# Seven small reorderings in a convolution and MLP-mixer kernel: token load order, weight passes, swap copies, output stores and background work

## Chip, cores and metric

The kernel runs on one core of a Trainium2 chip. The metric is the device time of one execution in microseconds (us), the median of several runs. Smaller is better.

## What is computed

The input x has 8 batches of 4096 tokens with 192 channels. A causal convolution with 7 taps per head (8 heads of 24 channels, taps passed through a softmax) goes first, and an MLP mixer follows:

```python
out = np.einsum('hk,bskhg->bshg', w, x_unf)            # convolution over tokens, softmaxed taps
xt = x.transpose(0, 2, 1)                              # x is now the convolution's output
h = np.maximum(xt @ w_tok1, 0.0) @ w_tok2              # token mixing: 4096 -> 256 -> 4096
u = x + h.transpose(0, 2, 1)
h2 = np.maximum(u @ w_ch1, 0.0) @ w_ch2                # channel mixing: 192 -> 1536 -> 192
return (u + h2).astype(np.float32)
```

The weights come in as 64-bit floats and are decoded on the chip into fp32 values. Products keep fp32 precision by a split: each operand is a high and a low part, and hi x hi, hi x lo and lo x hi are summed in PSUM.

## The kernel before, in words

**Groups and tiles.** Batches go in the groups [0], [1], [2, 3], [4, 5], [6, 7] (`GROUPS`, line 16). A group's tokens are cut into 8 spans of 512 tokens (`NT`), each of 4 blocks of 128 (`TJ`). In the groups of two batches, "pair groups" below, a span gives one tile per batch, worked one after the other as a pair.

**One tile.** The second token product (`mix2`) and the convolution's output give `u`. `u` is transposed into `own_hi` and `own_lo`, channels on partitions. Product 1 (`channel1`, matmuls in `channel1_mm`, line 1240) has 6 passes p of 18 matmuls on half the array each (108 in all). Each pass fills two PSUM tiles; ScalarE writes `hh`, the relu'd high part (line 1284), VectorE the low part `hl` (line 1285), and that frees the two PSUM tiles for a later pass. Product 2 has four blocks j: `channel2` (lines 1321, 1322) or, on half arrays, `channel2_halves` (line 1302). After each block VectorE adds products and `u` into `osb` (lines 1327, 1328, or 1308, 1310). `store_out` (line 1335) then sends `osb`, 384 KB for the tile, from POOL's queue. There is one `osb` buffer: the next tile's first write to it waits for the store to land.

**The pair's transposes** go by DMA. `blocks_sent` sends 16 block copies (line 1180). `parted` then casts the three chunks into `own_hi` (line 1192, ScalarE) and `own_lo` (line 1194, VectorE). It also makes a version with its halves of 64 partitions swapped: two ScalarE copies of 64x1536 (line 1197, high part, then low part) and two DMAs on POOL's queue (line 1199). Product 1 takes its weights' two half arrays from `own` and the swapped copy. A POOL memset (line 816) follows each load of raw input.

**Background.** While a group is mixed, the next group is convolved and sent through its first token product. A planner (`Background`, line 35) puts these instructions among the foreground's. `fg(pe, dve, after)` adds a foreground step's planned cost and fills in background items; `after` (600 unless given) says how far VectorE's plan may run ahead of TensorE's. Taps of the convolution are line 824 (first tap, ScalarE) and line 826 (the others, VectorE); raw loads are line 814, loads of decoded token weights line 877 (`t1_load`), stores of convolved tokens line 860. `bg.lands` plans when a load has landed.

**The start.** The first tiles of batch 0 run while weights are decoded on VectorE and ScalarE (lines 199 to 241): `begin(n)` starts the load of piece n, `chains[n]` are its decode steps, `split(n)` gives the high part (ScalarE) and the low part (VectorE). `hooks[0]` is the first tile's second token product. `load_tile` issues the loads of the next tile's `u` (line 1050) on SP's queue.

Of the kernel before, what the change touches and what calls it, by code (L numbers as in the profile page):

```python
# [142 lines left out]
def conv_mixer_kernel(ctx: ExitStack, tc: tile.TileContext, x, weight, w_tok1, w_tok2, w_ch1, w_ch2, out):  # L143
# [26 lines left out]
    def f32(ap):  # L170
        return ap.bitcast(F32)
# [169 lines left out]
    def woven(*lists):  # L341

        lists = [list(v) for v in lists]
        while any(lists):
            for v in lists:
                if v:
                    v.pop(0)()
# [95 lines left out]
    def stage1_first(pe, p0, p1, pd, late, load_u, after, pieces, hooks):  # L443
# [221 lines left out]
        def split(n):  # L665
            jb = jobs[n]
            hi, lo = jb["make"]() if "make" in jb else (jb["hi"], jb["lo"])
            return dec.b(sts[n], hi, lo, jb.get("view", lambda v: v))

        next_load()  # L670
        x0_load(0)
# [57 lines left out]
        low = split(N1)  # L729
        woven(chains[N1 + 1][:2])  # L730
        woven(low)
        held = []
        begin(N1 + 2, held)
        hooks[0]([lambda: None, lambda: None, chains[N1 + 1][2]])
        woven(chains[N1 + 1][3:])
        woven(chains[N1 + 2][:1])
        next_load()
        xc_store(1)
# [52 lines left out]
    def stage1(gi, pools):  # L791
# [44 lines left out]
        def begin(q2, part):  # L836
            def fn():
                states[q2]["raw", part] = load(q2, part)
                if nb > 1:
                    done["load", q2, part] = bg.lands(9e3)  # L840
                else:
                    mark("load", q2, part)

            bg.transfer(fn)
# [143 lines left out]
        convolving.append(Item(lambda: begin(0, 0), eager=True))  # L988
        second = [Item(lambda: begin(0, 1), eager=True, gate=lambda: None if pools(1) is None else 0.0)]
        for n in range(AHEAD[nb]):  # L990
            mixing.append(Item(lambda n=n: t1_load(n), eager=True))
        for q2 in range(NS):

            tap(q2, 0, 0)
# [114 lines left out]
    def mix2_half(t2, u, j, turned):  # L1109

        n = 2 * D
        pss = [ps_x.tile([P, TT], F32, name="ps_x") for _ in range(2)]
        prods = [(kc, r, v) for kc in range(KC) for r, v in ((0, 0), (0, 1), (1, 0))]
        for m, (kc, r, v) in enumerate(prods):
            for k, ps in enumerate(pss):
                ks = slice(k * D2, (k + 1) * D2)
                nc.tensor.matmul(  # L1117
                    out=ps[:, :n], lhsT=t2[ks, kc, r, j, :], rhs=h1[ks, kc, v, :n], start=m == 0, stop=m == len(prods) - 1
                )
        bg.fg(1040, 1070, 200)  # L1120
        uj = u[:, j]
        for ps in pss:
            v = ps[:, :n].rearrange("p (b c d) -> p c b d", b=2, d=D2)
            nc.vector.tensor_tensor(out=uj, in0=v, in1=uj, op=ALU.add)
        turn_blocks(uj, turned, j)
# [58 lines left out]
    def parted(place, other):  # L1184


        own = own_tile("hi"), own_tile("lo")
        low, high = slice(0, D2), slice(D2, P)
        for c in range(ND):
            v = f32(place[:, c]).rearrange("p (i j e) -> p j i e", i=NQ, e=QB)  # L1190
            hi, lo = (o[:, c].rearrange("p (j i e) -> p j i e", i=NQ, e=QB) for o in own)
            nc.scalar.copy(out=hi, in_=v)
            bg.fg(0, 700, 0)
            nc.vector.tensor_tensor(out=lo, in0=v, in1=f32(hi), op=ALU.subtract)
        swapped = other[:, 0], other[:, 1]
        for k in range(2):
            nc.scalar.copy(out=swapped[k][high], in_=f32(own[k][low]))  # L1197
        for k in range(2):
            nc.gpsimd.dma_start(out=f32(swapped[k][low]), in_=f32(own[k][high]))
        return [(own, swapped), (swapped, own)]  # L1200
# [71 lines left out]
    def channel1(t):  # L1272
        h = {}
        for f0 in range(0, NF, NF // 3):
            for n in ("hh", "hl"):
                part = hp.tile([P, NF // 3, TT], F32R, name=f"{n}{f0}")
                for f in range(NF // 3):
                    h[n, order[f0 + f]] = part[:, f]
        bg.tiled = True
        for p in range(NP):  # L1280
            pss = channel1_mm(t, p)
            bg.fg(2040 if p else 2400, 1300)
            for f, ps in pss:
                nc.scalar.activation(out=h["hh", f], in_=ps, func=AF.Relu)  # L1284
                nc.vector.scalar_tensor_tensor(  # L1285
                    out=h["hl", f], in0=ps, scalar=0.0, in1=f32(h["hh", f]), op0=ALU.max, op1=ALU.subtract
                )
        bg.tiled = False
        return h
# [182 lines left out]
    for gi, bs in enumerate(GROUPS):  # L1472
# [13 lines left out]
        for q in range(NT):  # L1486
            nxt = (gi, q + 1) if q + 1 < NT else (gi + 1, 0)
            for i, b in enumerate(bs):
# [30 lines left out]
                if spread and not turn:  # L1519

                    def after(j, z=spread[0], place=spread[1], t2=loaded[0], v=loaded[1]):
                        if j == 1:
                            bg.hold()
                        mix2_half(t2, v, j, z)
                        if j == TJ - 1:
                            blocks_sent(z, place)
                            bg.release()

                    channel2_halves(i, h, u, osb, range(TJ), after)
                    store_out(gi, b, q, osb, range(TJ), nc.gpsimd)  # L1530
                    continue
                if spread:
                    made = []
# [27 lines left out]
                product2 = channel2 if turn or last and q + 1 == NT and i + 1 == nb else channel2_halves  # L1561
                if ahead:
                    product2(i, h, u, osb, half[0])
                if turn and not pairs and ahead:
                    abc, rest = transposed_once(loaded[1])
                run_ahead(gi)
                if last and q + 1 == NT and i + 1 == nb:
                    for j in range(TJ):
                        if j in half[1]:
                            channel2(i, h, u, osb, [j])  # L1570
                        store_out(gi, b, q, osb, range(j, j + 1), nc.sync)
                else:
                    if ahead:
                        if turn and pairs:
                            made = []
                            channel2(i, h, u, osb, half[1], ((half[1][0], 7), lambda: made.extend(parted(other[:, 1], other))))
                            abc = made
                        elif turn:
                            channel2(i, h, u, osb, half[1], ((half[1][0], 7), rest))
                        else:  # L1580
                            product2(i, h, u, osb, half[1])
                    else:
                        made = []
                        first_channel2(u, osb, [3], (NF // 3, lambda: made.extend(transposed(loaded[1]))))
                        abc = made
                        second_split()
                        first["parted"] = 0.0
                        bg.dve = max(bg.dve, bg.pe) + 6e3

                    store_out(gi, b, q, osb, range(TJ), nc.gpsimd if ahead else nc.scalar)  # L1590
                if not ahead:
                    ht_ctx.close()
                    hp = ctx.enter_context(tc.tile_pool(name="hp", bufs=1, reuse_waits="tile"))
                if turn:
                    u = loaded[1]
                    if nxt[1] + 1 < NT:
                        loaded = load_tile(nxt[0], nxt[1] + 1, sp)


# [29 lines left out]
```

## Time and profile before

| | us |
|---|---|
| median of 3 runs (2006.88 to 2008.21) | 2007.21 |
| profiled execution, time | 2009.77 |
| profiled execution, span | 2008.0 |
| TensorE busy in the span | 1999.5 |
| VectorE busy | 1506.4 |
| ScalarE busy | 787.9 |
| POOL busy | 213.6 |

The granted clock of TensorE has the mean 1.0 over the span. Busy times are of the profiled execution and overlap: TensorE is busy nearly all the time, so only its few pauses can be won or lost, and the span is read as TensorE's work plus those pauses.

### The profile page before, as it was taken

To read this page: it belongs to the slowest core of one execution; us is meant where nothing else is said; L and a number is where in the kernel's file an instruction comes from. 1 tells how busy PE (TensorE), PEld (TensorE's weight loads), DVE (VectorE), ACT (ScalarE), POOL (GpSimd) and SP (SyncE) were. 2 spreads that over 40 slices of the span, in tenths; PEclk is the share of its full clock that TensorE was granted. 3 is DMA by queue.
4 is the path that set the end of the run, shared out by engine and by line. 5 is a ranking of instruction groups with operands and counts; after the bars stand their busy time and mean duration, and the time that the engine had idled before them with its cause. 6 is when DMAs were issued, how large, how long until landed. Compare 5 with 4: busy or idle time off the path is not lost.

```text
span 2008.0 us, 45327 instructions
## 1 busy us (share of the span) xinstructions
PE 1999.5 (100%) x19007; PEld 1853.6 (92%) x19007; DVE 1506.4 (75%) x3020; ACT 787.9 (39%) x1310; POOL 213.6 (11%) x376
## 2 busy tenths in 40 slices
PE   9999999999999999999999999999999999999999
PEld 9899999999988999998999999999999999999998
DVE  6899989999558999757888789556666666666664
ACT  7667544444343343323333433333233322333322
POOL 1000000000011101111101110111111110011110
PEclk9999999999999999999999999999999999999999
DMA  9956455553354567515346544433323222333310
GB/s 305 298 155 219 142 173 175 172 191 134 114 160 121 143 176 205 157 58 140 84 129 189 140 128 115 137 87 86 85 63 82 71 66 63 82 85 85 85 48 17
DMA packets 281792, 259.26 MB, mean 129 GB/s; under 512 B 190084, under 2 KB 231620, under 8 KB 281588
## 3 DMA queue, kind: packets, MB, share of 16 engines
q1 hardware_dynamic: 258404, 172.85, 30.6%
q0 software_dynamic: 22656, 83.12, 13.6%
q8 instruction: 150, 2.46, 0.5%
q14 instruction: 54, 0.44, 0.1%
q10 hardware_dynamic: 528, 0.39, 0.1%
HBM read 147.25 MB, written 71.30 MB: 109 GB/s over the span
## 4 chain that ended last, share of the span: by engine, by line
PE 92%; DVE 4%; DMA 2%; ACT 1%; SPq 1%; issue 0%; POOL 0%; DVEq 0%; ACTq 0%; POOLq 0%
PE ps_x L1240 37%; PE ps_x L1302 25%; PE ps_x L1321 10%; PE ps_x L1322 5%; PE ps_x L1117 3%; PE ps_a L932 2%; PE ps_a L933 2%; PE ps_a L934 2%; PE ps_x L1087 1%; PE ps_a L928 1%; DVE xc L826 1%; PE ps_x L1090 1%; DMA dec_raw<-in_moe_w_tok_dram 1%; PE ps_x L1092 1%; PE ps_x L1091 1%; PE ps_x L1161 1%
## 5 line engine op out<-in xcount | busy, mean ns | idle before, releaser
L1284 ACT ACTIVATE hh<-ps_x 128x512 fp32r<-128x512 f32 x756 | 410.2, 595 | 834.1 <-PE ps_x L1240 834.1
L1285 DVE SCALAR_TENSOR_TENSOR hl<-ps_x,hh 128x512 fp32r<-128x512 f32 x756 | 484.6, 686 | 172.1 <-ACT hh L1284 171.6
L1302 PE MATMUL ps_x<-w,hh 64*128 64x384 f32 x3648 | 523.5, 355 | 0.0
L1302 PE MATMUL ps_x<-w,hl 64*128 64x192 f32 x3648 | 462.3, 247 | 0.1
L1240 PE MATMUL ps_x<-other,w_hi 64*128 64x512 f32 x1728 | 448.7, 388 | 0.6 <-ACT other L1197 0.3
L826 DVE SCALAR_TENSOR_TENSOR xc<-raw,cw,xc 128x384 f32<-128x384 f32 (+1 forms) x768 | 389.1, 562 | 9.9 <-ACT xc L824 9.9
L1302 PEld LDWEIGHTS ps_x<-w,hl 64*128 64x128 f32 x3648 | 356.5, 188 | 2.1 <-DVE hl L1285 0.6
L1302 PEld LDWEIGHTS ps_x<-w,hh 64*128 64x128 f32 x3648 | 350.5, 184 | 1.5
L1240 PE MATMUL ps_x<-own_hi,w_hi 64*128 64x512 f32 x1440 | 348.7, 392 | 1.6 <-ACT w_hi L240 0.7
L1321 PE MATMUL ps_x<-w,hh 128*128 128x384 f32 x1200 | 348.1, 361 | 0.0
L1240 PEld LDWEIGHTS ps_x<-other,w_hi 64*128 64x128 f32 x1728 | 315.1, 184 | 32.6 <-ACT other L1197 1.0
L1240 PE MATMUL ps_x<-own_hi,w_lo 64*128 64x512 f32 x1440 | 343.2, 387 | 0.0
L1240 PE MATMUL ps_x<-own_lo,w_hi 64*128 64x512 f32 x1440 | 342.8, 387 | 0.2 <-ACT own_lo L1168 0.2
L1322 PE MATMUL ps_x<-w,hl 128*128 128x192 f32 x1200 | 300.4, 250 | 0.0
L1240 PEld LDWEIGHTS ps_x<-own_hi,w_hi 64*128 64x128 f32 x1440 | 214.7, 184 | 31.9 <-issue 4.2
L1240 PEld LDWEIGHTS ps_x<-own_lo,w_hi 64*128 64x128 f32 x1440 | 219.4, 184 | 26.7 <-ACT own_lo L1168 0.6
L1240 PEld LDWEIGHTS ps_x<-own_hi,w_lo 64*128 64x128 f32 x1440 | 219.3, 184 | 26.0
L1240 PE MATMUL ps_x<-other,w_lo 64*128 64x512 f32 x864 | 242.0, 386 | 0.0
L1322 PEld LDWEIGHTS ps_x<-w,hl 128*128 128x128 f32 x1200 | 229.1, 191 | 0.0
L1321 PEld LDWEIGHTS ps_x<-w,hh 128*128 128x128 f32 x1200 | 225.3, 188 | 0.5 <-DVE hl L1285 0.4
L1310 DVE TENSOR_TENSOR osb<-ps_x,osb 128x192 f32<-128x192 f32 x456 | 163.1, 358 | 26.8 <-DVE osb L1310 0.5
L1240 PEld LDWEIGHTS ps_x<-other,w_lo 64*128 64x128 f32 x864 | 159.0, 184 | 16.2
(190 smaller groups left out, 2025.5 us busy)
## 6 DMA issues: line engine op xcount, KB each, us to landing
raw<-in_x_dram SPq DMA_DIRECT2D x56, 672.0 KB, 8.1
t<-t2d SPq DMA_DIRECT2D x64, 512.0 KB, 5.4
out_dram<-osb POOLq DMA_DIRECT2D x62, 384.0 KB, 4.1
xcd<-xc POOLq DMA_DIRECT2D x28, 768.0 KB, 8.2
u<-xcd SPq DMA_DIRECT2D x56, 384.0 KB, 5.8
t<-t1p SPq DMA_DIRECT2D x32, 512.0 KB, 6.2
other<-own_hi POOLq DMA_DIRECT2D x24, 384.0 KB, 4.0
other<-own_lo POOLq DMA_DIRECT2D x24, 384.0 KB, 3.7
```

The costliest lines, as they stand in the source:

```text
L826: nc.vector.scalar_tensor_tensor(out=dst, in0=src, scalar=cw[:, h, k:k + 1], in1=dst, op0=ALU.mult, op1=ALU.add)
L932: nc.tensor.matmul(out=ps, lhsT=wh, rhs=xh, start=a, stop=False)
L933: nc.tensor.matmul(out=ps, lhsT=wh, rhs=xl, start=False, stop=False)
L934: nc.tensor.matmul(out=ps, lhsT=wl, rhs=xh, start=False, stop=z)
L1117: nc.tensor.matmul(out=ps[:, :n], lhsT=t2[ks, kc, r, j, :], rhs=h1[ks, kc, v, :n], start=m == 0, stop=m == len(prods) - 1)
L1240: nc.tensor.matmul(out=ps, lhsT=w1[w][rows, chunks[h][c], p * P:(p + 1) * P], rhs=t[h][v][rows, c], start=n == 0, stop=n == len(prods) - 1,)
L1284: nc.scalar.activation(out=h["hh", f], in_=ps, func=AF.Relu)
L1285: nc.vector.scalar_tensor_tensor(out=h["hl", f], in0=ps, scalar=0.0, in1=f32(h["hh", f]), op0=ALU.max, op1=ALU.subtract)
L1302: nc.tensor.matmul(out=ps[:, :m], lhsT=h[part, f][ks, ts], rhs=w2[ks, f, :m], start=n == 0 and part == "hh", stop=z and part == "hl",)
L1310: nc.vector.tensor_tensor(out=osb[:, j], in0=v, in1=osb[:, j], op=ALU.add)
L1321: nc.tensor.matmul(out=ps[:, :2 * D], lhsT=h["hh", f][:, ts], rhs=w2[:, f, :], start=n == 0, stop=False)
L1322: nc.tensor.matmul(out=ps[:, :D], lhsT=h["hl", f][:, ts], rhs=w2[:, f, :D], start=False, stop=z)
```

## The change

**A.** The third piece of the channel weights (`split(N1 + 2)`) is cast to its high part in two halves of its columns instead of in one cast. **B.** The first tile's second token product (`hooks[0]`) is issued before the third piece's decode begins, and not woven with it. **C.** For the first raw loads of the last group the planner takes 12 us to landing instead of 9. **D.** The first five loads of token weights for batch 1 (`t1_load`) wait, in the order of issue, until the third tile's tokens have been issued. **E.** The swapped high part is copied in three chunks of 64x512 instead of one copy of 64x1536, and the first pass of product 1 takes its matmuls chunk by chunk (hi x hi, hi x lo of a chunk, then all lo x hi). **F.** In product 1 of pairs the planner's `after` is 300 instead of 600. **G.** In pair groups the output of the pair's first tile, and in the last groups a tile that has the next pair's token product inside it, is stored in two halves of 192 KB, the first one after block j = 1.

```diff
--- before.py
+++ after.py
@@ -665,7 +665,13 @@
             hi, lo = jb["make"]() if "make" in jb else (jb["hi"], jb["lo"])
-            return dec.b(sts[n], hi, lo, jb.get("view", lambda v: v))
+            view = jb.get("view", lambda v: v)
+            if n != N1 + 2:
+                return dec.b(sts[n], hi, lo, view)
+            v = view(sts[n]["top"])
+            for cs in (slice(0, P), slice(P, 2 * P)):
+                nc.scalar.copy(out=hi[:, :, cs], in_=v[:, :, cs])
+            return [lambda: nc.vector.tensor_tensor(out=lo, in0=v, in1=f32(hi), op=ALU.subtract)]
 
@@ -729,10 +735,10 @@
         woven(low)
+        hooks[0]([])
         held = []
         begin(N1 + 2, held)
-        hooks[0]([lambda: None, lambda: None, chains[N1 + 1][2]])
-        woven(chains[N1 + 1][3:])
+        woven(chains[N1 + 1][2:])
         woven(chains[N1 + 2][:1])
@@ -837,7 +843,7 @@
                 if nb > 1:
-                    done["load", q2, part] = bg.lands(9e3)
+                    done["load", q2, part] = bg.lands(12e3 if gi == 4 and not q2 else 9e3)
                 else:
@@ -988,7 +994,7 @@
         for n in range(AHEAD[nb]):
-            mixing.append(Item(lambda n=n: t1_load(n), eager=True))
+            mixing.append(Item(lambda n=n: t1_load(n), eager=True, gate=lambda: first.get("later")))
         for q2 in range(NS):
@@ -1193,8 +1199,9 @@
         swapped = other[:, 0], other[:, 1]
-        for k in range(2):
-            nc.scalar.copy(out=swapped[k][high], in_=f32(own[k][low]))
+        for c in range(ND):
+            nc.scalar.copy(out=swapped[0][high, c], in_=f32(own[0][low, c]))
+        nc.scalar.copy(out=swapped[1][high], in_=f32(own[1][low]))
         for k in range(2):
@@ -1278,8 +1285,8 @@
         for p in range(NP):
-            pss = channel1_mm(t, p)
-            bg.fg(2040 if p else 2400, 1300)
+            pss = channel1_mm(t, p, by_chunk=not p and len(t) == 2)
+            bg.fg(2040 if p else 2400, 1300, 600 if t[0] is t[1] else 300)
             for f, ps in pss:
@@ -1522,12 +1529,14 @@
                         mix2_half(t2, v, j, z)
+                        if j == TJ // 2 - 1:
+                            store_out(gi, b, q, osb, half[0], nc.gpsimd)
                         if j == TJ - 1:
...
                     channel2_halves(i, h, u, osb, range(TJ), after)
-                    store_out(gi, b, q, osb, range(TJ), nc.gpsimd)
+                    store_out(gi, b, q, osb, half[1], nc.gpsimd)
                     continue
@@ -1561,6 +1570,8 @@
                     product2(i, h, u, osb, half[0])
+                    if turn and pairs:
+                        store_out(gi, b, q, osb, half[0], nc.gpsimd)
                 if turn and not pairs and ahead:
@@ -1587,7 +1598,8 @@
 
-                    store_out(gi, b, q, osb, range(TJ), nc.gpsimd if ahead else nc.scalar)
+                    js = half[1] if turn and pairs else range(TJ)
+                    store_out(gi, b, q, osb, js, nc.gpsimd if ahead else nc.scalar)
                 if not ahead:
@@ -1595,6 +1607,8 @@
                         loaded = load_tile(nxt[0], nxt[1] + 1, sp)
+                    if not ahead:
+                        first["later"] = 0.0
```

SP's queue at the start of batch 0's third tile (`raw` is raw input of the next batch, `u` the third tile's tokens, `t` token weights), before:

```order
L262 DMA dec_raw<-in_moe_w_tok_dram 128x1024 x2
L814 DMA raw_788<-in_x_dram 128x14x96
L814 DMA raw_791<-in_x_dram 128x14x96
L877 DMA t_794<-t1d 128x512
L877 DMA t_796<-t1d 128x512
L877 DMA t_798<-t1d 128x512
L877 DMA t_800<-t1d 128x512
L877 DMA t_802<-t1d 128x512
L1050 DMA u<-xcd_75 128x192 x4
L262 DMA dec_raw<-in_moe_w_tok_dram 128x1024 x3
```

and with the change:

```order
L262 DMA dec_raw<-in_moe_w_tok_dram 128x1024 x2
L820 DMA raw_789<-in_x_dram 128x14x96
L820 DMA raw_792<-in_x_dram 128x14x96
L1056 DMA u<-xcd_75 128x192 x4
L883 DMA t_947<-t1d 128x512
L883 DMA t_949<-t1d 128x512
L883 DMA t_951<-t1d 128x512
L883 DMA t_953<-t1d 128x512
L883 DMA t_955<-t1d 128x512
L262 DMA dec_raw<-in_moe_w_tok_dram 128x1024 x3
```

The four loads of `u` go ahead of the five loads of `t`. Lines have shifted by 6.

VectorE in the first pair's second tile, from the first write to `osb` to block j = 2 of product 2 (the bracket lists the semaphores that an instruction waits for; DMASW are POOL's DMAs), before:

```order
L1308 TENSOR_TENSOR osb<-ps_x,u 128x192 [waits DMASW4_49,PE_49]
L1310 TENSOR_TENSOR osb<-ps_x,osb 128x192 [waits DVE_49]
L1310 TENSOR_TENSOR osb<-ps_x,osb 128x192 [waits DVE_49,PE_49]
L1310 TENSOR_TENSOR osb<-ps_x,osb 128x192 [waits DVE_49]
L826 SCALAR_TENSOR_TENSOR xc_6810<-raw_6615,cw,xc_6810 128x16x24 x2
L826 SCALAR_TENSOR_TENSOR xc_6810<-raw_6615,cw,xc_6810 128x16x24 [waits DVE_49] x2
L1308 TENSOR_TENSOR osb<-ps_x,u 128x192 [waits PE_49]
L1310 TENSOR_TENSOR osb<-ps_x,osb 128x192 [waits DVE_49]
L1310 TENSOR_TENSOR osb<-ps_x,osb 128x192 [waits DVE_49,PE_49]
...
L826 SCALAR_TENSOR_TENSOR xc_6810<-raw_6615,cw,xc_6810 128x16x24 x2
L1308 TENSOR_TENSOR osb<-ps_x,u 128x192 [waits PE_49]
```

and with the change:

```order
L1315 TENSOR_TENSOR osb<-ps_x,u 128x192 [waits DMASW5_49,DMASW2_49,PE_49]
L1317 TENSOR_TENSOR osb<-ps_x,osb 128x192 [waits DVE_49]
L1317 TENSOR_TENSOR osb<-ps_x,osb 128x192 [waits DVE_49,PE_49]
L1317 TENSOR_TENSOR osb<-ps_x,osb 128x192 [waits DVE_49]
L832 SCALAR_TENSOR_TENSOR xc_6814<-raw_6616,cw,xc_6814 128x16x24 x2
L832 SCALAR_TENSOR_TENSOR xc_6814<-raw_6616,cw,xc_6814 128x16x24 [waits DVE_49] x2
L1315 TENSOR_TENSOR osb<-ps_x,u 128x192 [waits PE_49]
...
L832 SCALAR_TENSOR_TENSOR xc_6814<-raw_6616,cw,xc_6814 128x16x24 x2
L832 SCALAR_TENSOR_TENSOR xc_6814<-raw_6616,cw,xc_6814 128x16x24 [waits DVE_49] x2
L1315 TENSOR_TENSOR osb<-ps_x,u 128x192 [waits PE_49]
```

The first write to `osb` waits for both halves of the store before it, in place of one store, and two more taps (line 826, 832 with the change) stand ahead of block j = 2.

VectorE two pairs later, from the casts of the low part to the first pass of product 1, before:

```order
L1194 TENSOR_TENSOR own_lo<-other,own_hi 128x512 [waits Activation_49] x2
L826 SCALAR_TENSOR_TENSOR xc_8386<-raw_8344,cw,xc_8386 128x16x24 x2
L1327 TENSOR_TENSOR osb<-ps_x,u 128x192 [waits PE_49]
L1328 TENSOR_TENSOR osb<-ps_x,osb 128x192 [waits DVE_49]
L826 SCALAR_TENSOR_TENSOR xc_9176<-raw_9012,cw,xc_9176 128x16x24 [waits DMAHW1_49,DMAHW0_49,Activation_49]
...
L1327 TENSOR_TENSOR osb<-ps_x,u 128x192 [waits PE_49]
L1328 TENSOR_TENSOR osb<-ps_x,osb 128x192 [waits DVE_49]
L916 TENSOR_TENSOR xhl<-xc_8386,xhl 128x768
L826 SCALAR_TENSOR_TENSOR xc_9176<-raw_9012,cw,xc_9176 128x16x24 x2
L1285 SCALAR_TENSOR_TENSOR hl_9209<-ps_x,hh_9208 128x512 [waits Activation_49] x4
```

and with the change:

```order
L1200 TENSOR_TENSOR own_lo<-other,own_hi 128x512 [waits Activation_49] x2
L1334 TENSOR_TENSOR osb<-ps_x,u 128x192 [waits PE_49]
L1335 TENSOR_TENSOR osb<-ps_x,osb 128x192 [waits DVE_49]
L832 SCALAR_TENSOR_TENSOR xc_9189<-raw_9024,cw,xc_9189 128x16x24 [waits DMAHW1_49,DMAHW0_49,Activation_49]
L832 SCALAR_TENSOR_TENSOR xc_9189<-raw_9024,cw,xc_9189 128x16x24 [waits Activation_49]
...
L1334 TENSOR_TENSOR osb<-ps_x,u 128x192 [waits PE_49]
L1335 TENSOR_TENSOR osb<-ps_x,osb 128x192 [waits DVE_49]
L922 TENSOR_TENSOR xhl<-xc_8361,xhl 128x768
L1292 SCALAR_TENSOR_TENSOR hl_9222<-ps_x,hh_9221 128x512 [waits Activation_49] x2
L832 SCALAR_TENSOR_TENSOR xc_9189<-raw_9024,cw,xc_9189 128x16x24 x2
L1292 SCALAR_TENSOR_TENSOR hl_9222<-ps_x,hh_9221 128x512 [waits Activation_49] x2
```

Two taps behind the casts and two ahead of the first pass's `hl` are gone from here; of the four `hl` of two passes, two now go before the next taps.

## Rows read from the trace of the kernel before

**Rows 1.** The page, part 4.
```profile
PE 92%; DVE 4%; DMA 2%; ACT 1%; SPq 1%; issue 0%; POOL 0%; DVEq 0%; ACTq 0%; POOLq 0%
```

**Rows 2.** The chain that ended last; start us, us, what ran or landed.
```profile
102.47 4.70 DMA u<-xcd
...
602.08 6.81 PE ps_x L1302 x96
...
620.73 8.68 PE ps_x L1240 x71
...
1534.06 12.28 PE ps_x L1240 x108
```

**Rows 3.** Timeline of SP's queue at 92 to 105 us; start us, us, instruction.
```profile
91.91 4.67 SPq L814 DMA_DIRECT2D raw<-in_x_dram  x2
96.62 5.75 SPq L877 DMA_DIRECT2D t<-t1d  x5
102.47 2.03 SPq L1050 DMA_DIRECT2D u<-xcd  x4
```

**Rows 4.** Timeline of VectorE at four places; brackets: idle before, releaser.
```profile
107.27 0.36 DVE L1102 TENSOR_TENSOR u<-ps_x,u 128x192 f32<-128x192 f32 x1 [1.93 <-DMA u<-xcd]
...
608.89 0.36 DVE L1308 TENSOR_TENSOR osb<-ps_x,u 128x192 f32<-128x192 f32 x1 [2.75 <-PE ps_x L1302]
...
616.30 0.75 DVE L1310 TENSOR_TENSOR osb<-ps_x,osb 128x192 f32<-128x192 f32 x2 [0.46 <-DVE osb L1310]
...
781.70 1.14 DVE L826 SCALAR_TENSOR_TENSOR xc<-raw,cw,xc 128x384 f32<-128x384 f32 x2
782.76 2.48 DVE L1285 SCALAR_TENSOR_TENSOR hl<-ps_x,hh 128x512 fp32r<-128x512 f32 x4
```

**Rows 5.** Timeline of TensorE at 59 to 128 us.
```profile
59.89 0.98 PE L1240 MATMUL ps_x<-own_hi,w_hi 64*128 64x512 f32 x6 [0.72 <-ACT w_hi L240]
...
94.85 1.56 PE L1240 MATMUL ps_x<-own_hi,w_hi 64*128 64x512 f32 x6 [0.34 <-DVE hl L1285]
...
118.77 0.73 PE L1240 MATMUL ps_x<-own_hi,w_hi 64*128 64x512 f32 x4
...
127.59 0.62 PE L1240 MATMUL ps_x<-own_hi,w_hi 64*128 64x512 f32 x2
```

**Rows 6.** Timeline of TensorE at 647 to 924 us.
```profile
647.77 0.49 PE L1240 MATMUL ps_x<-other,w_hi 64*128 64x512 f32 x1
...
712.53 0.50 PE L1240 MATMUL ps_x<-other,w_hi 64*128 64x512 f32 x1
...
783.50 0.48 PE L1240 MATMUL ps_x<-own_hi,w_hi 64*128 64x512 f32 x1
784.09 0.50 PE L1240 MATMUL ps_x<-other,w_hi 64*128 64x512 f32 x1
...
922.66 0.36 PE L1302 MATMUL ps_x<-w,hh 64*128 64x384 f32 x2
...
923.90 0.88 PE L1117 MATMUL ps_x<-h,t 64*128 64x384 f32 x8
```

**Rows 7.** Timeline of ScalarE at six places.
```profile
73.53 1.15 ACT L199 ACTIVATE t_first<-dec_raw 128x1024 f32<-128x1024 f32 x1 [3.21 <-DMA dec_raw<-in_moe_w_tok_dram]
...
119.73 0.62 ACT L1167 CAST own_lo<-own_lo 64x512 fp32r<-64x512 f32 x1
...
586.30 1.66 ACT L1192 CAST own_hi<-other 128x512 fp32r<-128x512 f32 x3 [14.38 <-DMA other<-own_hi]
...
646.25 1.48 ACT L1197 CAST other<-own_hi 64x1536 fp32r<-64x1536 f32 x1
...
706.79 1.47 ACT L1197 CAST other<-own_lo 64x1536 fp32r<-64x1536 f32 x1
...
920.65 1.12 ACT L824 ACTIVATE xc<-raw,cw 128x384 f32<-128x384 f32 x2 [1.57 <-POOL raw L816]
```

**Rows 8.** DMA issues from 595 to 599 us; KB each, us to landing.
```profile
out_dram<-osb POOLq DMA_DIRECT2D x1, 384.0 KB, 11.8
```

## Prediction

> **What bounds the kernel now.** I read the chain of waits first. It lies on TensorE for 92% of the span [rows 1], and late in the run its pieces are whole products: a product 1 of 108 matmuls in 12.28 us, 0.1137 us each [rows 2]. That is the pace without a pause, so nothing gains there. What the change can win is the pauses of TensorE in the first half. I looked for them by comparing starts in TensorE's timeline with this pace, and then read the timeline of the engine each pause waits for. Five places matter, and each is met by one or two of the seven edits. The reader should see in the rows who was late there.
>
> - **At 119 to 128 us** 66 matmuls run between two starts, 118.77 and 127.59 [rows 5]. At the pace they take 7.50, so 1.32 us are pauses. VectorE is in arrears there since 107.27, where it had stood for 1.93 us until the third tile's `u` landed [rows 4]. That landing is in the chain [rows 2], and its issue on SP stands behind five loads of token weights that took 5.75 us to issue [rows 3].
> - **At 619 us** a product 1 begins when 192 matmuls of product 2 are over, from 602.08 at 6.81 for 96, that is at 615.70. It ends at 629.41 [rows 2], 13.71 instead of 12.28: 1.4 us of pause. VectorE stood for 2.75 us before 608.89 [rows 4]. The row names TensorE as releaser. I take it to be the store of the one `osb` instead: it was issued between 595 and 599 and took 11.8 us [rows 8], so it landed close to 608.89, and this instruction is the first write to `osb`.
> - **At 647 us** TensorE goes on at 647.77 [rows 6], as the first swap copy ends, 646.25 + 1.48 [rows 7].
> - **At 784 us** two starts lie 0.59 apart, 783.50 and 784.09 [rows 6], where 0.23 is the pace of two half arrays: 0.36 us. It waits for a PSUM buffer that `hl` at 782.76 frees, and that stands behind two taps [rows 4].
> - **At 923 us** from 922.66 to 923.90 two steps of product 2 pass [rows 6]. A step is 4 of the matmuls that take 6.81 for 96, 0.284, so 0.67 is pause. ScalarE had stood 1.57 us on raw input before a tap at 920.65 [rows 7], with the last `hh` of that product 1 behind it.
>
> **The change part by part.**
>
> A and B: 0. TensorE's 0.72 us at 59.89 waits for the cast that A cuts in two, and B brings the first tile forward. But at 94.85 TensorE waits for `hl` on VectorE [rows 5], whose work there began with a landing of weights that ScalarE awaited for 3.21 us at 73.53 [rows 7]. What is won before only lengthens that wait. If the landing moves with the edits, since its load is issued behind the decode, it is up to 0.7 either way.
>
> D: -1.3. With four loads of `u` ahead of the five, they are issued at 96.62 and not at 102.47; with the same 4.70 to landing [rows 2, 3] `u` is there at 101.3. VectorE came free at 105.34, so its whole 1.93 us go, more than the 1.32 of pauses behind it. Of these I take all. The other end is 0: the two raw loads issued just before [rows 3] are in the same queue, and if they hold `u` beyond 107 nothing is won. The five loads are issued 2.03 later; the next batch's token product that needs them comes after the convolution, which covers that, and without the cover it costs 2.03 at most.
>
> G: 0 at 609. The first `osb` write waits for both halves, the buffer is waited for as a whole. The second half is issued on POOL behind the same two swap DMAs as the whole store before, and the queue has the same bytes to bring. So I take the same landing, 608.9. Bounds: the 2.75 us vanish, or the half lands later. One more POOL issue in each of 24 pairs is hidden: POOL is busy for 213.6 us of the span in all, and what it issues behind the second half is the next pair's.
>
> F at 619: +0.6. The order shows two more taps ahead of block j = 2, 1.06 from start to start of such a pair and what follows [rows 4]. VectorE stood 0.46 within that block [rows 4], which takes some in; 0.60 is left, and TensorE's pause ends with VectorE. Between 0, if TensorE is later itself, and 1.06.
>
> E at 588 and 647: +0.4 at the second only. Three chunk copies replace one of 1.48 [rows 7]. The nearest row with 64 partitions and 512 columns is a cast of 0.62, three are 1.86: +0.4. Three casts of 128 partitions in a run took 1.66 [rows 7]: +0.2. I take the first, for its partitions. The chunked first pass can start earlier, but six of its nine steps (1.36 us) later it needs the low copy, and that now ends 0.4 later. So the early start is a wait moved. At 588 the same delay sits before the store's wait at 609, which takes it in. In the other 22 pairs the copies are done well ahead: for the pair at 712.53 [rows 6] the low copy ends at 708.26 [rows 7], 4.3 us before.
>
> F at 784: -0.4. The pair of taps ahead of `hl` goes, 1.06, more than the 0.36 of pause. The taps come later, where VectorE has product 1 as cover; without it they would cost the 0.36 again.
>
> C at 923: -0.65. The taps go behind the last `hh` and `hl`, and the 0.67 with them. They may then press on product 2's first `osb` write, so it is between 0 and -0.67.
>
> Sum: -1.3 + 0.6 + 0.4 - 0.4 - 0.65 = **-1.35 us**. The profiled execution took 2009.77 (span 2008.0, 1.8 lie around it), 2.6 over the median; it would come to 2008.4, and the median 2007.21 to **2005.8**.
>
> By the rule in the Trainium skill, DMA: Bandwidth & Descriptors, section Anatomy of one DMA — SWDGE (gpsimd) path, a store of this kind takes 2.0 us plus its bytes at 436 GB/s. An estimate from that page is 2.9 us for 384 KB and 2.5 for a half. The trace disagrees by a factor of four for this store, with 11.8 us [rows 8]; by the page's figure the first rival below would be the case.
>
> **The rivals.**
>
> 1. The last half lands early and the wait at 609 goes. For it: the first half is out before the swap DMAs, and 192 KB are left behind them. Against: all went through one queue, and the order in it, not the size of the last piece, set the landing. It takes the 1.4 us at 619 and F's 0.6 with it, brings E's 0.4 at 588 to light, and the transposes of the next pair come earlier, so that E's 0.4 at 647 is covered: -1.3 - 1.4 + 0.4 - 0.4 - 0.65 = -3.35, about 2003.9; with E's cheap price and some of 647's pause gone, 2003.
>
> 2. D doesn't do what it says: `u` lands no earlier, because the raw loads hold the queue. For it, raw is issued for 4.67 us just ahead [rows 3]. Against: between those and `u` five loads were taken out. The sum is then -0.05, 2007.2.
>
> 3. A and B carry through to 94.85: -0.7 more, 2005.1.
>
> 4. Slower: the second half store lands later than the whole one did, as two more DMAs share the queue with loads of the next group. Each us after 608.9 delays VectorE's `osb` writes and TensorE by one us. It decides from 5.4 us on, a landing after 614.3: six us late give 2011.8. Against: the same bytes go through the same queue, and late in the run TensorE at its pace [rows 2] leaves no such wait.
>
> **How the numbers follow.** 0.2%, 4.0 us, is about what a measurement of this kernel can tell from no change: below 2003.2 is faster, above 2011.2 slower. Forecast 0.45, first rival 0.25, second 0.15, third 0.1, fourth 0.05. Faster needs the first rival with cheap copies, or together with the third, and some gain in places that I price at nothing: 0.26. Slower is the fourth and a little for what I have not seen: 0.06. The same: 0.68. The range of 8 in 10 goes from the first and third rival together with cheap copies (2003.9 - 0.7 - 0.4 = 2002.8, and 0.4 for the pause at 647) to the second with F at its dear end (+0.46): 2002.4 to 2007.7.
>
> **What would show it.** D: VectorE's wait for `u` at 107 is gone, and TensorE's 66 matmuls behind take 7.5 us. G: the first `osb` write of the first pair's second tile still stands near 609. F: the product 1 behind it takes about 14.3 us. E: the first pass starts without a pause and stops after six steps. F and C: no pause at 784 and at 923. A prompt `osb` write at 606 would prove the forecast wrong and the first rival right; a pause at 125 as long as before, the second.

## The result, and the profile after

The changed kernel takes 2017.54 us in the median of 6 runs (2015.78 to 2021.1), the kernel before 2007.44 on the same chip: a ratio of 1.0051, 95% interval [1.004, 1.0062]. It is slower by ten us where the forecast was 1.35 us faster. The profiled execution took 2016.4, span 2014.6.

A table of stretches shows where. The row that matters, with the columns: stretch, its length, busy time of TensorE (instructions), of its weight loads, VectorE, ScalarE and POOL, the granted clock, DMA share, GB/s. First the kernel before, then the changed one:

```profile
760.00:800.00 40.00, 39.89 (x364) 37.12 (x363) 36.30 (x71) 16.70 (x27) 7.83 (x13) 1.00 0.83 235
```

```profile
760.00:800.00 40.00, 32.93 (x257) 30.65 (x257) 27.75 (x52) 16.41 (x29) 8.38 (x14) 0.91 0.80 230
```

These 40 us lose 6.96 us of TensorE's work, and the granted clock falls to 0.91 in the mean. In the other stretches looked at (100 to 130, 700 to 760, 800 to 1200 and 1200 to 1900 us) TensorE is busy all the time and the clock 1.00; of 560 to 650 it is busy for 89.18 us, 89.26 before. So this is not a cost spread over 24 pairs of tiles; it is one event, at the place that the prediction calls 784. TensorE's timeline there (start, length, instruction, in brackets idle time and releaser):

```profile
775.92 0.50 PE L1247 MATMUL ps_x<-own_hi,w_hi 64*128 64x512 f32 x1
...
780.13 0.39 PE L1247 MATMUL ps_x<-own_hi,w_hi 64*128 64x512 f32 x1
787.59 0.76 PE L1247 MATMUL ps_x<-other,w_hi 64*128 64x512 f32 x1 [7.07 <-DVE osb L1335]
...
788.15 0.62 PE L1247 MATMUL ps_x<-other,w_hi 64*128 64x512 f32 x1
...
790.85 0.39 PE L1247 MATMUL ps_x<-other,w_hi 64*128 64x512 f32 x1
```

TensorE stands 7.07 us in the middle of a product 1, until VectorE's second `osb` write (line 1335) has read a PSUM tile. The granted clock falls within the pause: it is 1.00 up to 782, 0.50 from 784 to 790.2, and 1.00 again from 791. So behind the pause TensorE goes on at the lower of its two clock levels (1.2 GHz): a matmul lasts 0.62 in place of 0.39, and from 787.59 to 790.85 eight steps take 3.26 where the pace of two half arrays, 0.23, gives 1.84. The pause has a second price of 1.4 us.

The chain of waits says what held VectorE:

```profile
765.20 0.53 SPq L820
...
765.77 14.89 DMA raw<-in_x_dram
...
780.75 0.62 ACT xc L830
...
781.39 5.38 DVE xc L832 x10
...
787.08 0.37 DVE osb L1335
...
787.59 9.75 PE ps_x L1247 x71
```

It is read from below. The `osb` write stands on VectorE behind ten taps; the taps wait for ScalarE's first tap (line 830); that waits for raw input, whose load took 14.89 us. In the kernel before, the same ten taps stood ahead of the same write. There ScalarE's tap and VectorE's taps and writes were:

```profile
774.22 2.14 ACT L824 ACTIVATE xc<-raw,cw 128x384 f32<-128x384 f32 x4
```

```profile
774.87 5.38 DVE L826 SCALAR_TENSOR_TENSOR xc<-raw,cw,xc 128x384 f32<-128x384 f32 x10 [1.74 <-ACT xc L824]
...
780.55 0.36 DVE L1328 TENSOR_TENSOR osb<-ps_x,osb 128x192 f32<-128x192 f32 x1
```

They ended at 780.91. TensorE's product 1 began at 777.25 there. In the changed kernel the matmul that waits belongs beside the one at 780.13, on the other half of the array: 4.21 after the start at 775.92. In the kernel before, the matmul at that place ran at 781.47, 4.22 after the start:

```profile
777.25 0.50 PE L1240 MATMUL ps_x<-own_hi,w_hi 64*128 64x512 f32 x1
...
781.47 0.39 PE L1240 MATMUL ps_x<-other,w_hi 64*128 64x512 f32 x1
```

The cover was 0.6 us wide (781.47 - 780.91). Taps that start 6.5 us later (780.75 against 774.22) go through it.

**Why the load is late.** SP's queue and POOL's, before:

```profile
766.99 1.41 SPq L814 DMA_DIRECT2D raw<-in_x_dram  x2
771.88 3.56 SPq L890 DMA_DIRECT2D t<-t1p  x2
775.54 8.31 SPq L814 DMA_DIRECT2D raw<-in_x_dram  x2
```

```profile
770.82 0.54 POOL L1199 DMA_DIRECT2D other<-own_hi  x1 [5.02 <-ACT own_hi L1192]
771.70 0.53 POOL L1199 DMA_DIRECT2D other<-own_lo  x1 [0.34 <-DVE own_lo L1194]
772.76 1.84 POOL L860 DMA_DIRECT2D xcd<-xc  x2 [0.53 <-DVE osb L1327]
```

and with the change:

```profile
765.20 14.78 SPq L820 DMA_DIRECT2D raw<-in_x_dram  x4
780.07 2.62 SPq L896 DMA_DIRECT2D t<-t1p  x2
```

```profile
766.86 1.78 POOL L866 DMA_DIRECT2D xcd<-xc  x2
769.16 0.55 POOL L1206 DMA_DIRECT2D other<-own_hi  x1 [0.52 <-ACT own_hi L1198]
770.05 0.53 POOL L1206 DMA_DIRECT2D other<-own_lo  x1 [0.34 <-DVE osb L1334]
```

Two steps moved that no edit names. On POOL the store of convolved tokens (`xcd`, two DMAs of 768 KB) now goes ahead of the pair's swap DMAs, 1.7 us after the raw load was issued and not 5.8. On SP the second pair of raw loads goes ahead of two loads of `t1p`. Both come from F. As I read the planner, with `after` at 300 it finishes the convolved span earlier, and what follows a finished span, its store and the next load, is put in earlier too. Experiment 2 shows the same new order with F alone.

What the queues moved meanwhile (queue and kind: packets, MB, share of 16 engines; q0 is POOL's, q1 is SP's), for 772 to 776 us with the change:

```profile
q0 software_dynamic: 349, 1.46, 92.1%
q1 hardware_dynamic: 352, 0.13, 12.1%
```

and in the kernel before for 769 to 772 us, where SP's queue has the engines to itself:

```profile
q1 hardware_dynamic: 2480, 0.95, 114.2%
```

Packets of the two queues went one for one, but POOL's hold 4.2 KB in the mean (1.46 MB / 349) and those of the raw load 0.37 KB. The load crawled at 0.03 MB per us, a tenth of the 0.32 that q1 had alone. The Trainium skill, DMA: Bandwidth & Descriptors, section Queues, rings and completion order, says that a DMA engine takes turns between its queues packet by packet; 349 against 352 agrees.

### The profile page after: what moved, and what is told of

It is laid out like the page before. It is cut to its first block, busy times and chain, and to the rows that moved or that the text cites. A ratio compares the mean times of both kernels' runs of the same rounds, so it can differ in the third digit from the quotient of the medians.

```text
span 2014.6 us, 45419 instructions
## 1 busy us (share of the span) xinstructions
PE 1998.9 (99%) x19007; PEld 1859.8 (92%) x19007; DVE 1505.7 (75%) x3020; ACT 792.9 (39%) x1359; POOL 227.0 (11%) x400
## 4 chain that ended last, share of the span: by engine, by line
PE 91%; DVE 4%; DMA 3%; SPq 1%; ACT 1%; issue 0%; POOL 0%; ACTq 0%; DVEq 0%; POOLq 0%
PE ps_x L1247 37%; PE ps_x L1309 25%; PE ps_x L1328 10%; PE ps_x L1329 5%; PE ps_x L1123 3%; PE ps_a L938 2%; PE ps_a L939 2%; PE ps_a L940 2%; PE ps_x L1093 1%; PE ps_a L934 1%; DVE xc L832 1%; DMA raw<-in_x_dram 1%; DVE hl L1292 1%; DMA dec_raw<-in_moe_w_tok_dram 1%; PE ps_x L1096 1%; PE ps_x L1167 1%
## 5 line engine op out<-in xcount | busy, mean ns | idle before, releaser
L1247 PE MATMUL ps_x<-other,w_hi 64*128 64x512 f32 x1728 | 464.5, 388 | 7.6 <-DVE osb L1335 7.1
L1247 PE MATMUL ps_x<-own_hi,w_hi 64*128 64x512 f32 x1440 | 362.4, 392 | 2.0 <-DVE hl L1292 1.1
L1247 PE MATMUL ps_x<-own_hi,w_lo 64*128 64x512 f32 x1440 | 358.2, 387 | 0.0
L1247 PE MATMUL ps_x<-other,w_lo 64*128 64x512 f32 x864 | 258.0, 387 | 0.0
```

What stands on the lines that cost most here:

```text
L1247: nc.tensor.matmul(out=ps, lhsT=w1[w][rows, chunks[h][c], p * P:(p + 1) * P], rhs=t[h][v][rows, c], start=n == 0, stop=n == len(prods) - 1,)
```

## The experiments

**Theory S**: the store that goes ahead of the swaps starves the raw load. **R**: it is the second raw pair, which goes ahead of the `t1p` loads. Others are named in the expectations. Each experiment is a short diff against the changed kernel or the one before.

**1. All edits but F** (`f_undone`)

```diff
-            bg.fg(2040 if p else 2400, 1300, 600 if t[0] is t[1] else 300)
+            bg.fg(2040 if p else 2400, 1300)
```

> The change with F alone undone (600 again). In the trace of the change TensorE stands for 7.3 us at 780 us behind taps that wait for a raw load, and the order shows that F alone moves that load's neighbours: the store of the convolved tokens on POOL's queue ahead of the swap DMAs, and a second pair of raw loads ahead of token weights on SP's. Theory S (the store starves the load) and theory R (the second pair of raw loads holds it): both undone here, TensorE's pause at 780 is under 1 us, and the time is the kernel before's less what the other edits win, 2003 to 2005.5. Theory H (the half stores of G or the chunk copies of E press on the queues): the pause stays, 2015 to 2019.

2007.96 (2007.09 to 2009.0, 11 runs), ratio 1.0001 [0.9992, 1.001]. The loss is gone with F, but the gain that was expected of the other edits isn't there: the time lies above 2003 to 2005.5. Product 1's rows on TensorE show what stands at that place now:

```profile
780.95 0.49 PE L1247 MATMUL ps_x<-own_hi,w_hi 64*128 64x512 f32 x1
781.55 0.49 PE L1247 MATMUL ps_x<-other,w_hi 64*128 64x512 f32 x1
```

A start 0.60 behind the last, as in the kernel before [rows 6]: the small pause that F was priced to remove.

**2. F alone** (`f_alone`): the kernel before with the one line of F.

> The kernel before with F alone. Theories S and R: the pause at 780 comes with it, 6 to 9 us with the slow clock behind it, 2013 to 2017. Theory H: no pause, 2006 to 2008.5.

2017.94 (2016.68 to 2020.33, 5 runs), ratio 1.0047 [1.0035, 1.006]. Its POOL issues the store at 765.10, ahead of the swaps at 768.63. The raw load is issued at 765.00, the tap on it starts at 780.26, and TensorE stands for 7.1 us:

```profile
765.10 1.82 POOL L860 DMA_DIRECT2D xcd<-xc  x2 [1.17 <-DVE osb L1327]
768.63 0.54 POOL L1199 DMA_DIRECT2D other<-own_hi  x1 [1.71 <-ACT own_hi L1192]
```

F is the whole loss; chunk copies, halves and the load order have no part in it.

**3. That one store behind the swaps** (`store_behind`)

```diff
             done["storing", q2] = True
-            bg.transfer(fn)
+            if gi == 3 and q2 == 2:
+                first["behind"] = fn
+            else:
+                bg.transfer(fn)
...
             nc.gpsimd.dma_start(out=f32(swapped[k][low]), in_=f32(own[k][high]))
+        if "behind" in first:
+            first.pop("behind")()
```

> The whole change, with one store of convolved tokens (2 x 768 KB on POOL's queue) issued behind the next two swap DMAs in place of ahead of them, as in the kernel before; VectorE's and SP's order are the change's. Theory S: the raw load lands 7 to 10 us after its issue and not 15, the pause at 780 is under 1.5 us, 2003.5 to 2007. Theory R: the load still takes 14 us or more, the pause stays, 2015 to 2019.

2008.16 (2006.53 to 2009.67, 10 runs), ratio 0.9999 [0.999, 1.0008]. All else of the change is as it was, the second raw pair too. SP's queue, ScalarE's tap and VectorE's ten taps:

```profile
763.03 7.43 SPq L820 DMA_DIRECT2D raw<-in_x_dram  x4
```

```profile
771.56 2.14 ACT L830 ACTIVATE xc<-raw,cw 128x384 f32<-128x384 f32 x4
```

```profile
772.20 5.38 DVE L832 SCALAR_TENSOR_TENSOR xc<-raw,cw,xc 128x384 f32<-128x384 f32 x10 [2.92 <-ACT xc L830]
```

From issue to tap it takes 8.5 us and not 15.6. One store of 1.5 MB, moved past two DMAs in POOL's order, is worth the ten us. S is shown: the store's place decides. Its median lies above 2003.5 to 2007, as in experiment 1 without a gain from the other edits.

**4. The second raw pair behind two loads of `t1p`** (`raw_behind`)

```diff
+            if gi == 3 and q2 == 3 and part == 1:
+                first["late raw"] = [2, fn]
+            else:
+                bg.transfer(fn)
...
             mark("t1", n)
+            if gi == 3 and "late raw" in first:
+                first["late raw"][0] -= 1
+                if not first["late raw"][0]:
+                    first.pop("late raw")[1]()
```

> The whole change, with the second pair of raw loads issued behind two loads of token weights in place of ahead of them, as in the kernel before; VectorE's and POOL's order are the change's. Theory S: the first pair still lands 13 us or more after its issue, the pause stays at 5 to 8 us, 2013 to 2018. Theory R: it lands within 10 us, the pause is under 1.5 us, 2003.5 to 2007.

2017.45 (2010.52 to 2018.59, 5 runs), ratio 1.0038 [1.0025, 1.0051]. SP's order is that of before again, yet the tap on the first pair, issued at 766.86, starts 15.4 us later:

```profile
782.28 2.13 ACT L830 ACTIVATE xc<-raw,cw 128x384 f32<-128x384 f32 x4 [8.14 <-DMA raw<-in_x_dram]
```

R is wrong. One of the five executions took only 2010.52, with a granted clock of 1.0 in the mean where the other four had 0.997 or 0.998. It has no trace; how late the store makes the load can differ from execution to execution.

**5. The planner told that this load takes longer** (`later_taps`)

```diff
-                    done["load", q2, part] = bg.lands(12e3 if gi == 4 and not q2 else 9e3)
+                    done["load", q2, part] = bg.lands(12e3 if gi == 4 and not q2 else 16e3 if gi == 3 and q2 == 3 else 9e3)
```

> The whole change, with the planner's landing estimate at 16 us instead of 9 for the raw loads of one span (group [4, 5], the last span), so that its ten taps are planned behind the first pass's hl on VectorE and no longer ahead of an osb write. The store stays ahead of the swaps. Theory S: the load still lands about 15 us after its issue, but what frees PSUM no longer stands behind it, so the pause at 780 is under 2 us: 2005 to 2009. Theory L (the late load holds ScalarE's hh as well, so any order waits for it): a pause of 4 us or more stays, 2012 to 2017.

2007.73 (2005.6 to 2009.77, 11 runs), ratio 0.9997 [0.9988, 1.0006]. The loads are as slow as ever (15.0 us from issue to landing in the median of the four, 14.8 with the change), but the taps no longer stand ahead of the `osb` write:

```profile
775.72 0.36 DVE L1334 TENSOR_TENSOR osb<-ps_x,u 128x192 f32<-128x192 f32 x1 [5.57 <-PE ps_x L1329]
```

So a slow load costs nothing by itself. It costs because instructions that wait for it stand ahead of the ones that free PSUM: in the changed kernel VectorE stood for 10.98 us before its ten taps, with the `osb` write behind them. ScalarE's first taps stood ahead of the first `hh` there (780.75, `hh` at 782.78), and this edit moved them too (783.04, behind an `hh` at 782.07), so what each of the two engines adds is not separated. Experiments 3 and 5 cut the same chain at its two ends.

**6 and 7. The kernel before, profiled twice more** (`before_again`, `before_third`). No edit.

> The kernel before once more, for a second trace. Theory V (its pauses at 125, 588, 619, 647, 784 and 923 hang on DMA landings and differ from execution to execution, so that what the six other edits win in one trace is not won in the median): at least two of the six are gone or under half. Theory C (they recur): all six within 0.3 us of the first trace.

> The kernel before, a third trace; the same two theories and numbers.

2006.98 and 2007.06, one execution each. The pauses that the prediction counted are not fixtures. The first `osb` write that stood 2.75 us [rows 4] stood 1.02 in the second trace, and did not wait in the third:

```profile
606.57 0.36 DVE L1308 TENSOR_TENSOR osb<-ps_x,u 128x192 f32<-128x192 f32 x1 [1.02 <-DMA out_dram<-osb]
```

```profile
605.50 0.35 DVE L1308 TENSOR_TENSOR osb<-ps_x,u 128x192 f32<-128x192 f32 x1
```

Before the tap at 920.65 [rows 7], where ScalarE stood for 1.57 us, it stands for 0.95 and 1.17 in these two (917.87 and 917.95). The releaser of that `osb` write in the second trace is the store of `osb`, as the prediction read it against the row of the first. The first trace took 2009.77, some 2.6 us over the median, and these pauses are part of that surplus.

**8. D and C alone** (`d_and_c`): the kernel before with the gate on `t1_load` and the 12 us estimate.

> The kernel before with D and C alone, the two edits priced at -1.3 and -0.65. Theory C (the pauses they remove recur): 1.5 to 2.5 us under the kernel before, 2005.3 to 2006.3. Theory V: within 1 us of it.

2007.6 (2006.54 to 2010.2, 11 runs), ratio 1.0 [0.9991, 1.0008]. This lies 0.28 under the kernel before, as theory V has it, and outside theory C's range. The two edits whose gain the trace bears out (below) are not seen in the median: together they were priced at 1.95 us, at the edge of an interval that reaches about 1.8 to either side. A gain of half of that can't be told from none here.

**9. The store cut into column halves** (`small_packets`): four DMAs of 384 KB in place of two of 768.

```diff
+                parts = [slice(0, D // 2), slice(D // 2, D)] if gi == 3 and q2 == 2 else [slice(0, D)]
                 for i in range(nb):
-                    nc.gpsimd.dma_start(out=xcd[gi][:, i, q2 * RB:(q2 + 1) * RB], in_=xc[:, :, i])
+                    for cs in parts:
+                        nc.gpsimd.dma_start(out=xcd[gi][:, i, q2 * RB:(q2 + 1) * RB, cs], in_=xc[:, :, i, cs])
```

> The whole change, with the one store of convolved tokens that goes ahead of the swaps cut into column halves (4 x 384 KB, rows of 384 bytes instead of 768 side by side); place and bytes are the change's. In the trace of the change, from 772 to 776 us, POOL's queue moved 349 packets with 1.46 MB and SP's 352 with 0.13 MB. Theory T (the two queues take turns by packet, so large packets starve the raw load's small ones): with small packets the load lands 7 to 12 us after its issue, the pause at 780 is under 2.5 us, 2004 to 2010. Theory B (the bytes of the store on the queue ahead decide): it lands after 13 us or more and the pause stays at 5 to 8 us, 2013 to 2018.

2016.62 (2016.29 to 2018.01, 4 runs), ratio 1.0043 [1.003, 1.0057]. It tells nothing on the size of packets, since it did not change it. In 772 to 776 us:

```profile
q0 software_dynamic: 340, 1.28, 95.5%
q1 hardware_dynamic: 338, 0.13, 13.3%
```

A packet of POOL's still holds 3.8 KB in the mean, and the turns are one for one again. Halved rows were put together into packets of nearly the old size: without the small ones under 512 B, 26 of POOL's packets with the change and 48 here, they hold 4.5 KB (1.46 MB / 323) and 4.4 (1.28 MB / 292). The Trainium skill, DMA: Bandwidth & Descriptors, section SWDGE vs HWDGE vs iDMA, gives 4096 B or less as the preferred size of a packet; these are somewhat larger. Whether smaller packets would let the load through stays open.

**10. One of the two stores behind the swaps** (`half_behind`): as experiment 3, but the first 768 KB stay ahead.

```diff
...
+                split = gi == 3 and q2 == 2
+                for i in range(1 if split else nb):
+                    send(i)
+                if split:
+                    first["behind"] = lambda: send(1)
...
```

`send(i)` issues store i of the two; the put-off one is issued behind the swaps as in experiment 3.

> The change with one of the two 768 KB stores of that span issued behind the next swap DMAs; the other stays ahead of them, as the change has both. Theory S in amounts (each store ahead of the swaps costs the raw load its part): between issue and landing the raw load took 14.9 us with both ahead and about 8.5 with none, so about 11.7 here; the tap on it near 776 to 777, the ten taps end near 782 to 783, and TensorE stands for 3 to 4 us near 780 in place of 7.3. Median 2011 to 2013. Rival A (any store ahead holds the load until it and the swaps are through): the load takes over 14 us and TensorE stands for 7 us; median 2016 to 2018. Rival N (one store fits into gaps): the load takes under 9.5 us, TensorE stands for under 1.5 us; median 2007 to 2008.5.

2015.88 (2014.07 to 2020.39, 5 runs), ratio 1.0036 [1.0022, 1.005]. Between theory S and rival A (any store ahead holds the load until it and the swaps are through), and nearer to A:

```profile
770.73 12.95 DMA raw<-in_x_dram
```

```profile
776.26 0.94 POOL L865 DMA_DIRECT2D xcd<-xc  x1
```

```profile
790.61 0.76 PE L1255 MATMUL ps_x<-other,w_hi 64*128 64x512 f32 x1 [4.84 <-DVE osb L1343]
```

The load took 12.95 us, not 11.7, and TensorE stood for 4.84. The second store was issued at 776.26, seven us before the load landed: what was put behind the swaps still met the load, so this was no clean half. The trace is of the slowest of the five executions, which had also lost five us before this place, so its pause does not give the median.

When the load lands speaks for A. With the change it lands at 780.66, and the second swap DMA, issued at 770.05 with 10.5 us to landing, at 780.5. In experiment 4 the two land at 782.20 and 781.9, here at 783.68 and 784.2. The load is done about when POOL's queue is through with the store and the swaps, and half a store less shortens it by only 1.9 us. This is read from three traces; in `f_alone` the load lands 1.4 us behind the swap. The direction is S's, and how much each part of POOL's queue costs isn't settled.

**11. Both cures** (`both_fixed`): experiments 3 and 5 together.

> The whole change with the store behind the swaps and the taps planned for a landing of 16 us. The pause at 780 and the one at 784 of the kernel before are gone: under 0.5 us together. If the rest of the change wins what its trace shows, 2004.5 to 2006.5; if that differs from execution to execution as the traces of the kernel before do, within 1 us of it.

2006.55 (2005.55 to 2009.26, 11 runs), ratio 0.9994 [0.9985, 1.0003]. The lowest median of all, but its interval holds 1. The product 1 in question runs without a pause, 108 matmuls at the pace of [rows 2] to within 0.2 us:

```profile
775.39 12.47 PE ps_x L1252 x108
```

## Why the prediction was wrong, step by step

**The step that failed** is "F at 784: -0.4. [...] The taps come later, where VectorE has product 1 as cover". It was worked out on VectorE's order alone. The order of POOL and SP had the store and the raw loads in new places, and the step did not price them: a step moved past two queues, with its DMAs uncounted. It also took cover for granted without measuring it. The rows of before give 0.6 us. By rows of both traces the place costs +8.1: product 1 begins 1.33 earlier than before (775.92 against 777.25), and a later one 6.81 later, in the chains of before and of the changed kernel:

```profile
842.80 12.47 PE ps_x L1240 x108
```

```profile
849.61 12.47 PE ps_x L1247 x108
```

The 8.1 are the pause, 7.46 between two starts less 0.23, and 1.4 for the clock, less about 0.5 that before lost there: from this product 1 to the next it took 26.50 us (777.25 to 803.75), where 26.00 is the time without a wait. What the step set out to remove, a pause behind two taps, was real and small; what it set off was twenty times its price.

**D, -1.3: right in the trace.** `u` is issued at 94.77 and the loads of `t` after it; VectorE's first `u` at 104.97 waits for nothing. The 66 matmuls take 7.62 us, from 119.25 to 126.87, against 8.82 before and 7.50 expected:

```profile
119.25 0.73 PE L1247 MATMUL ps_x<-own_hi,w_hi 64*128 64x512 f32 x4
...
126.87 0.39 PE L1247 MATMUL ps_x<-own_hi,w_hi 64*128 64x512 f32 x2
```

But this place varies, and the first trace had it at its dearest. From this product 1 to the next it took 30.89 us there, 29.91 and 30.00 in the two other traces of before, and 29.45 with the change: what D saves is 0.5 us in those two, not 1.3.

**A and B, 0: right in the mechanism, 0.5 off by a landing.** Half a microsecond was won: the product 1 of 88.06 began at 87.54. But the wait at 94.85 [rows 5] took it back and 0.46 more, as the landing that ScalarE awaits at 73.53 [rows 7] came 0.47 later:

```profile
74.00 1.15 ACT L199 ACTIVATE t_first<-dec_raw 128x1024 f32<-128x1024 f32 x1 [4.23 <-DMA dec_raw<-in_moe_w_tok_dram]
```

```profile
95.31 1.10 PE L1247 MATMUL ps_x<-own_hi,w_hi 64*128 64x512 f32 x3 [1.07 <-DVE hl L1292]
```

In twelve of the thirteen traces, with A and B and without, TensorE goes on there 21.30 to 21.34 us after ScalarE begins on this landing; the other (`f_undone`) has the earliest landing. The prediction had named a moving landing, as up to 0.7 either way. That the edits delay it is not shown: it came between 73.1 and 76.6 in the traces with them and between 73.4 and 75.8 in those without.

**G, 0 at 609, and F at 619, +0.6: not as priced.** The first `osb` write stood at 606.85, waiting 1.55 us for a half. That is half of the first rival: the halves landed before the 608.9 of the whole. The product 1 behind it takes 13.3 us (614.45 to 627.77), where before took 14.0 (615.32 to 629.34) and the forecast was 0.6 more. So 0.7 of the 1.4 us of pause went. The rest ends with VectorE:

```profile
606.85 0.36 DVE L1315 TENSOR_TENSOR osb<-ps_x,u 128x192 f32<-128x192 f32 x1 [1.55 <-DMA out_dram<-osb]
```

```profile
619.38 0.50 PE L1247 MATMUL ps_x<-own_hi,w_hi 64*128 64x512 f32 x1 [0.30 <-DVE osb L1317]
```

VectorE works from 606.85 to there without a stop, so F's two further taps may well be in it. In `f_alone`, where the store landed early and this write waited only 0.26 us, the same taps cost TensorE nothing. How much of the earlier landing is G's is open, since the whole store of before landed as early in its other two traces.

**E, +0.4 at 647: the low bound was right.** Three chunks take 1.66, and the low copy begins 1.56 behind the first of them; in the kernel before it began 1.38 behind the whole copy (770.56 to 771.94). That is +0.18. Priced from one cast alone (0.62), three come to 1.86; in a run they took 1.66. And it was a cost in this trace only as far as the copies were late: in `f_undone`, with the same chunks, TensorE had no pause at this place.

```profile
586.97 1.66 ACT L1203 CAST other<-own_hi 64x512 fp32r<-64x512 f32 x3
588.53 1.47 ACT L1204 CAST other<-own_lo 64x1536 fp32r<-64x1536 f32 x1
```

**C, -0.65: right in the trace.** The lag of 6.81 us before the place is 6.17 behind it (944.58 against 938.41) and stays so to the end. The taps stand behind the last `hh`. In the other two traces of before little was there to win: from the product 1 at 907 to the next it takes 30.34 and 30.56 us there, 30.96 in the first trace and 30.31 with the change.

**The rivals.** The fourth had the sign, but named another store, another place and a chance of 0.05. The first came half true, for 0.7 us. The second failed, as `u` landed in time; so did the third, as the wait at 94.85 grew. **The numbers** failed with F (2007.21 - 1.35 is 2005.9 and not 2005.8, which changes nothing): the range's top, 2007.7, left out the fourth rival, the only one with a price for a landing that moves. The rest of the sum has a fault of its own. Its pauses were read from one trace, 2.6 us over the median, and taken off the median; the kernels without the ten us (experiments 1, 3, 5 and 11) lie at 0.9994 to 1.0001 of before, and their intervals hold both no gain and the forecast one (0.9993).

## What to carry to other kernels

When a planner's parameter moves work, compare the order of every queue, those that only issue DMAs first: here the moved taps took a 1.5 MB store ahead of two DMAs of its own queue, and so onto a load on another queue. Wherever instructions that wait for a load stand ahead of the one that frees PSUM, work out how many us of cover there are; with 0.6 us, a landing that slipped by 6.5 stopped TensorE for seven, and the clock came on top. And take two more traces of the kernel before you price pauses under 1.5 us: of the five counted here, those at 619, 647 and 923 us were gone or under 0.3 in the next two executions, and the one at 119 to 128 was about 0.5 and not 1.3. Only the one at 784 came back in full.

## What the runs showed of the hardware

Two queues with work for the same engines had equal numbers of packets, 349 to 352 and 340 to 338, whatever these hold, so a load with packets of 0.37 KB got about a twelfth of the bytes beside a store with packets of over 4 KB. Cutting that store's rows in two left its packets at nearly the same size, 4.4 KB and not 4.5. And a pause of 7.07 us was followed by 2.7 us at the lower clock level, which added a fifth to its price (1.4 us). That addition is no constant: behind the same pause in `f_alone`, 71 matmuls took 10.77 us, a whole us more than the 9.75 above.
